# A state-space block and a gated two-layer network: the first weights held back, x issued between GpSimd's own work, and two pieces of weights in one transfer

## The chip, the cores and the metric

The kernel runs on one core of a Trainium2 chip. A core has five engines with instruction queues of their own: TensorE (PE in the profile, with its weight loads as PEld), VectorE (DVE), ScalarE (ACT), GpSimd (POOL) and SyncE (SP), which only issues transfers. Matrix products go to PSUM, everything else lies in SBUF. Transfers from and to the main memory can be issued by SP, ACT and POOL, and are carried by 16 DMA engines.

The metric is the device time of one execution in microseconds; lower is better. The kernel before was run three times: 350.02, 350.31 and 350.38 us, a median of 350.31.

## The reference

The first half is a state-space layer (Mamba-2's SSD) over 4 batches, 8 heads, 768 positions, head size 32 and state size 16, in chunks:

```python
cum = np.cumsum(log(clip(a, 1e-6, 1)), axis=-1)          # inside a chunk
M   = (C @ B^T) * exp(cum_i - cum_j) * causal            # scores, weighed
y   = M @ x  +  (C @ state) * exp(cum)                   # inside, and from earlier chunks
state = exp(sum) * state + sum_j B_j x_j exp(cum_last - cum_j)
```

The second half takes y as 3072 rows of 256 numbers:

```python
h = x @ w_in                        # 256 -> 2048
g = h * (1 / (1 + exp(-1.702 * h)))
out = g @ w_out                     # 2048 -> 256
```

The weights `w_in` and `w_out` come as float64; x, a, B and C as float32. The kernel works in float32.

## The kernel before, in words

The positions are cut into six groups of 128, and a group holds 512 rows of the second half (128 positions of 4 batches). A group consists of two pairs of batches (`PG` = 2), so pair 0 and pair 1 are the batches 0 and 1, and 2 and 3, of the first group. All instructions are written out in one order for each engine, and `in_order` at the end fixes that order; nothing is left to a scheduler but the waits between engines. The change lies in the first 25 us or so, where the first group's state-space part is computed and the first weights come in.

What that beginning consists of, with lines of the kernel before:

- **Loading a, C and B.** One copy of a (L273), eight transfers of C (SP and ACT), eight of B (three by SP, five by POOL; L130).
- **x of the two pairs** is loaded by POOL, two transfers of 128 KB for each pair (`load`, L146), behind POOL's constants: `ident`, `below`, and `pick`, which is one memset and four selects (L287 to L290).
- **Decays.** PE and ACT make `L`, the exponents of the differences of cumulated logarithms, pair 0 with one ACT instruction and pair 1 with four (L531). `drop_of` (L454, POOL) copies the last column of each L, from which `ends_first` (L460, VectorE) makes `Be`, B scaled with the decay to the end of the half chunk.
- **Turning and scores.** `turn_blocks` (L543, VectorE) turns C and B; `turn_back` (L557, PE) turns B back into a PSUM bank, from which `Be` is made; `score` (L599, PE) makes C times B into the area `cb`.
- **Weighing.** `weigh` (L610, VectorE) multiplies L with the scores in place, one half of a pair in an instruction (`k` = 0 and 1).
- **y.** `finish` and `gain` on PE: a dense filler matmul (L418), then products of the weighed L and x (L726, four sets of 16 for each pair), the state's increment from x and `Be` (L630), S on ACT (L646), the products with the state (L711), and the copies to `yT` on ACT (L738).
- **since_start** (L585, POOL) makes C scaled with the decay from the start, read by L711. `first` (L1077) is a POOL memset of a constant that is first read much later, by `clip_rows`.

The weights come in ten **pieces** (`PIECES`, L150): pieces 0 to 3 are two row blocks of 128 of `w_in` each (512 KB of float64), 4 and 5 four row blocks each (1 MB), 6 to 9 are `w_out`. `fetch` (L159) issues a piece as two transfers, one for each half of the inner dimension. Pieces 0 and 1 share a tile, and so do 2 and 3; there are four such tiles. With `held`, a one-element memset of the tile is put on VectorE ahead of the transfer, so that SP waits until VectorE has come to that place.

VectorE and ACT turn a piece into float32: `fields` (L189, L192) splits exponent and mantissa, `clamp` (L201, L203, ACT) moves the exponent, `rounded` (L207) adds the low word, `join` (L221, L227) puts sign, exponent and mantissa together into `w_in` or `w_out`. `narrow(i)` is `rounded(i)`, `fields(i + 1)`, `join(i)`. `join` also fetches a later piece (`NEXT`).

The hidden layer of the first group (`hidden`, L787) goes through 16 row blocks f, each of which needs its part of `w_in`: piece 0 for f = 0 and 1, piece 1 for 2 and 3, piece 2 for 4 and 5, piece 3 for 6 and 7, piece 4 for 8 to 11, piece 5 for 12 to 15. Between the row blocks stand the conversions of the later pieces (`narrow(3)` behind f = 3, `narrow(4)` behind f = 4) and the work of the second group. `az1` and `az` are two more copies of a (64 and 96 KB, L1089 and L1090), which POOL clips (`clip`, L362), and which `pick_a` (L374, ACT) and the store to a scratch area (L1120) read; behind the clips POOL issues the loads of C and B of the second group.

After the first group the kernel is an almost unbroken row of matmuls to the end.

Of the kernel before, what the change touches and what calls it, by code (L numbers as in the profile page):

```python
# [35 lines left out]
def kernel(  # L36
# [73 lines left out]
    cum = const.tile([P, 2, P], FP32, name="cum")  # L110
    w_in = const.tile([P, NF, NK, P], FP32, name="w_in")
    w_out = const.tile([P, 2, NF, P], FP32, name="w_out")
    rx, rb = {}, {}

    blocks = {}

# [17 lines left out]
    def load(p, parts=None, queue=nc.sync):  # L134
        if parts is None:
            parts = "bx"
            if p % PG == 0:
                for name in "CB":
                    load_blocks(p // PG, name, [nc.sync])
        for part in parts:  # L140
            dst, src, e = {"b": (rb, B, N), "x": (rx, x, D)}[part]
            dst[p] = raw.tile([P, 2, NH, e], FP32, tag=part, name=f"{part}{p}", bufs=3)
            for k in range(2):
                c, b = place(p)
                sl = slice(c * P, (c + 1) * P)
                queue.dma_start(out=dst[p][:, k], in_=src[b + k, :, sl, :].rearrange("h s d -> s h d"))  # L146
# [9 lines left out]
    def words(name):  # L156
        return wide.tile([P, 2 * PN], U32, tag="bits", name=name, bufs=BUFS)

    def fetch(i, queue=nc.sync, held=False):  # L159
        name, f, n = PIECES[i]  # L160
        if n == 2 and f % 4:
            t = pieces.pop(i - 1)[:, 2 * n * DM:]
        else:
            t = pieces[i] = words(f"bits{i}")
            t = t[:, :2 * n * DM]
        if held:
            nc.vector.memset(t[:, :1], 0)
        if name == "in":
            src = moe_w_in[:, 2 * f * P:2 * (f + n) * P].rearrange("(k p) e -> p k e", p=P)
            dst, src = (v.rearrange(s, h=n, e=2 * P) for v, s in (  # L170
                (t, "p (h k e) -> k p h e"), (src, "p k (h e) -> k p h e")))
        else:
            src = moe_w_out[f * P:(f + n) * P, :].rearrange("(f p) (h e) -> h p f e", p=P, h=2)
            dst = t.rearrange("p (h f e) -> h p f e", h=2, f=n)
        for k in range(2):
            queue.dma_start(out=dst[k], in_=src[k])  # L176
        t = t.rearrange("p (e w) -> p e w", w=2)
        bits[i] = t[:, :, 0], t[:, :, 1]

# [100 lines left out]
                                compare_op=ALU.is_ge, fill=-1e5, base=0,  # L282
                                channel_multiplier=-1)
    load_blocks(0, "B", [nc.gpsimd, nc.sync, nc.gpsimd, nc.sync, nc.gpsimd, nc.sync, nc.gpsimd, nc.gpsimd])
    fetch(0)
    pick = const.tile([P, NB, Q], FP32, name="pick")
    nc.gpsimd.memset(pick, 1.0)  # L287
    for r in range(R):
# [1 line left out]
        nc.gpsimd.affine_select(out=rows, in_=rows, pattern=[[-NH, NB], [-1, Q]],  # L290
                                compare_op=ALU.is_equal, fill=0.0, base=-Q * r,
                                channel_multiplier=1)
    for p in range(PG):
        load(p, "x", nc.gpsimd)
    early = const.tile([P, 1], FP32, name="early")
    nc.vector.memset(early, 1.0)

# [164 lines left out]
        BE[p] = t.rearrange("p r (k q) n -> p k r (q n)", k=2), t  # L462

    since = {}

    firsts = {}

    def clip_rows(g):
        t = raf[g]
# [49 lines left out]
    def decay_exp(p, r, t):  # L519

        n = 2 * Q * H
        if p not in flat:
            if r is None:
                L = ssd.tile([P, R, n], FP32, tag="L", name=f"L{p}", bufs=3)
            else:
                both = const.tile([P, R, n + P], FP32, name=f"L{p}")
                flat[p, "rows"], L = both, both[:, :, :n]
                since[0] = both[:, :, n:]
            flat[p] = L
            Ls[p] = L.rearrange("p r (k q i) -> p k r q i", k=2, q=Q)  # L530
        nc.scalar.activation(flat[p] if r is None else flat[p, "rows"][:, r], t, AF.Exp)  # L531
# [145 lines left out]
    def finish(pairs, steps=range(2)):  # L677


        g, first = divmod(pairs[0], PG)  # L680
        early = pairs[0] < PG
        if 0 in steps:
            if early:
                banks = begun_y["banks"] = [bank(f"y0_{i}") for i in range(4)]
                y = [t[:, :2 * P].rearrange("p (k i) -> p k i", i=H) for t in banks]
                begun_y[0] = [[y[2 * t + i] for t in range(NK)] for i in range(2)], set()
            else:
                both = area(f"y{pairs[0]}")[:, :, :len(pairs) * 2 * H].rearrange(
                    "p (s t) (k i) -> p s t k i", s=2, i=H)
                begun_y[pairs[0]] = [[both[:, i, t] for t in range(NK)] for i in range(2)] + [both], set()  # L690
        y, begun = begun_y[pairs[0]]

        def begin(i, t, parts):
            new = not begun & {(i, t, q) for q in parts}
            begun.update((i, t, q) for q in parts)
            return new

        def inter(n, p, ts=range(2)):

            b = place(p)[1]  # L700
            for k in range(2):
                for i in range(2):
                    if g == 0 and i == 0:
                        continue
                    old = (state[g][:, 0] if i else state[g - 1][:, 1])[:, b + k]
                    for r in range(R):
                        t = r // 2
                        if t not in ts:
                            continue
                        rows, to = slice(32 * r, 32 * r + 32), Q * D * (r % 2)  # L710
                        nc.tensor.matmul(  # L711
                            out=y[i][t][to:to + Q * D, 2 * n + k], lhsT=old[rows],
                            rhs=st[p]["CsT"][rows, k, SIDES[i]],
                            start=begin(i, t, range(Q * (r % 2), Q * (r % 2) + Q)), stop=early,
                            tile_position=(32 * r, to), skip_group_check=True)

        def intra(n, p):
            L = Ls[p]
            for k, t in [(k, t) for t in range(NK) for k in range(2)] if early else [
                    (k, t) for k in range(2) for t in range(NK)]:  # L720
                if p == 0 and (k, t) == (0, 1):
                    dense(begun_y["banks"][0][:, 2 * P:])
                for q in range(HB):
                    h = t * HB + q
                    for i, side in enumerate(SIDES):
                        nc.tensor.matmul(  # L726
                            out=y[i][t][D * q:D * q + D, 2 * n + k], lhsT=rx[p][side, k, h],
                            rhs=L[side, k, h // Q, h % Q],
                            start=begin(i, t, (q,)), stop=not early, tile_position=(H * i, D * q),
                            skip_group_check=True)  # L730

        cols = slice(2 * first * P, 2 * (first + len(pairs)) * P)

        if first == 0 and g not in yT:
            yT[g] = ffn.tile([P, NK, TG], FP32, tag="yT", name=f"yT{g}")
        if early:
            def copied(i, t):
                nc.scalar.activation(  # L738
                    yT[g][:, t, cols].rearrange("p (k s i) -> p s k i", s=2, i=H)[:, i], y[i][t],
                    AF.Copy)  # L740

            if 0 in steps:
                dense(begun_y["banks"][0][:, 2 * P:])
                intra(0, pairs[0])
                return
            intra(1, pairs[1])
            for t in range(NK):
                copied(0, t)
            for t in range(NK):
                for n, p in enumerate(pairs):  # L750
                    inter(n, p, (t,))
                copied(1, t)
        else:
            for step in steps:
                for n, p in enumerate(pairs):
                    (inter, intra)[step](n, p)
            if 1 not in steps:
                return
            for i in range(2):
                nc.scalar.activation(  # L760
                    yT[g][:, :, cols].rearrange("p t (k s i) -> p s t k i", s=2, i=H)[:, i], y[2][:, i],
                    AF.Copy)
        state.pop(g - 1, None)
        for p in pairs:
            st.pop(p)
            Ls.pop(p)
# [296 lines left out]
    turn_blocks(0, "C")  # L1063
    mask_blocks(1)
    decay_exp(0, None, both[:, :, :2 * Q * H])
    mask_first(0)
    differ_of(1)
    rows_first(seconds)
    for r in range(R):
        decay_exp(1, r, seconds[r][:, :3 * P])  # L1070
    table(AF.Silu)
    drop_of(0)
    drop_of(1)
    for p in range(PG):
        since_start(p, nc.gpsimd)
    firsts[0] = ssd.tile([P, NB, P], FP32, tag="first", name="first", bufs=1)
    nc.gpsimd.memset(firsts[0], 0.0)  # L1077
    turn_blocks(0, "B")
    turn_back()
    fold_ident(1)  # L1080
    score(range(PG))
    fields(0)
    clamp(0)
    for p in range(PG):
        ends_first(p)
    weigh(0, (slice(0, 1),))
    fetch(1, held=True)
    rows = a.rearrange("b h s -> (b h) s")
    nc.sync.dma_start(out=az1[:, 0], in_=rows[:, P:2 * P].unsqueeze(0).to_broadcast([R, NB * NH, P]))  # L1089
    nc.sync.dma_start(out=az.rearrange("p c s -> p (c s)"), in_=rows)  # L1090
    for t in az1, az:
        clip(t)
    weigh(0, (slice(1, 2),))
    for i in range(2, 6):
        fetch(i, held=i == 2)
    for k in range(2):
        weigh(1, (slice(k, k + 1),))
    rounded(0)
# [246 lines left out]
```

## Time and profile before

| | |
|---|---|
| median of three runs | 350.31 us |
| the profiled execution: its own time, its span | 350.15 us, 348.4 us |
| TensorE clock granted in it | 0.999 |
| PE busy | 341.9 us (98%) |
| VectorE busy | 256.5 us (74%) |
| ACT, POOL busy | 149.6 us (43%), 45.6 us (13%) |
| first matmul of the hidden layer (L787) | at 17.09 us |
| share of PE in the chain that ended last | 91% |

A busy PE is not a PE at its peak, since matmuls are pipelined and their ends are modelled. Rows of the timeline are: start in us from the beginning of the span, duration in us (of several instructions merged, from the first start to the last end), engine, line, operation, output and inputs with sizes, count, and in square brackets the idle time of the engine before the row with what ended it. Rows of the chain are start, duration and what; "issue" is time in which nothing that the profile shows was waited for. In the windows by stage, DMA throughput is given in GB/s.

### The profile page before, as it was taken

How to read it: one execution, taken by the hardware profiler on the slowest of the kernel's cores; microseconds unless marked ns; L12 is line 12 of the kernel's file. 1: busy time of each engine (PE TensorE's matmuls, PEld its weight loads, DVE VectorE, ACT ScalarE, POOL GpSimd, SP SyncE). 2: the span in 40 equal slices, each digit the busy share in tenths (PEclk: the TensorE clock that was granted, in tenths of full speed). 3: DMA queues.
4: the chain of work that ended last, by engine and by line, in shares of the span. 5: the costliest groups of instructions: out<-in, count | busy, mean ns of one | idle time of the engine just before them, and what ended most of it. 6: DMA issues, size and time to landing. Idle time of an engine off the chain costs nothing.

```text
span 348.4 us, 8535 instructions
## 1 busy us (share of the span) xinstructions
PE 341.9 (98%) x3514; PEld 280.4 (80%) x3514; DVE 256.5 (74%) x474; ACT 149.6 (43%) x333; POOL 45.6 (13%) x82
## 2 busy tenths in 40 slices
PE   8899999999999999999999999999999999999996
PEld 7557874545788888888888888888888888899996
DVE  7799999999699997839985648985554654455463
ACT  6759774005354313744342543433444321554320
POOL 8446500300495000000000000000000000000000
PEclk9999999999999999999999999999999999999999
DMA  5589984623639000464122326120000120000221
GB/s 137 171 267 312 297 156 129 93 57 73 103 76 149 2 0 13 84 121 92 27 36 58 49 79 120 23 33 8 2 2 2 19 32 11 1 2 0 33 31 60
DMA packets 82831, 25.79 MB, mean 74 GB/s; under 512 B 68856, under 2 KB 81144, under 8 KB 82792
## 3 DMA queue, kind: packets, MB, share of 16 engines
q1 hardware_dynamic: 79912, 23.19, 30.8%
q0 software_dynamic: 1888, 1.74, 2.3%
q8 instruction: 27, 0.44, 0.6%
q10 hardware_dynamic: 992, 0.33, 0.4%
q14 instruction: 12, 0.10, 0.1%
HBM read 21.99 MB, written 3.24 MB: 72 GB/s over the span
## 4 chain that ended last, share of the span: by engine, by line
PE 91%; POOL 2%; DMA 2%; DVE 2%; SPq 1%; issue 1%; POOLq 0%; DVEq 0%
PE acc L945 28%; PE X L843 19%; PE Y L853 14%; PE o L885 8%; PE h L787 7%; PE acc L952 7%; DMA bits<-in_moe_w_in_dram 2%; PE y L726 2%; PE cb L599 2%; PE y L711 2%; PE A L630 1%; POOL x L146 1%; SPq L176 1%; POOL zB L130 1%; DVE L L610 0%
## 5 line engine op out<-in xcount | busy, mean ns | idle before, releaser
L848 ACT ACTIVATE ac<-X 128x256 f32<-128x256 f32 x76 | 29.2, 384 | 79.8 <-PE X L843 79.4
L945 PE MATMUL acc<-mg,mw 128*128 128x256 f32 x192 | 54.5, 379 | 0.0
L972 DVE TENSOR_TENSOR gT<-Y,ac 128x512 f32<-128x512 f32 x38 | 26.2, 690 | 37.4 <-PE Y L853 33.6
L820 ACT ACTIVATE gT<-gT 128x512 f32<-128x512 f32 (+1 forms) x76 | 39.4, 521 | 31.7 <-DVE gT L972 31.1
L843 PE MATMUL X<-my,mi 128*128 128x256 f32 x152 | 45.1, 379 | 0.0
L972 DVE TENSOR_TENSOR gT<-Y,b 128x256 f32<-128x256 f32 x38 | 15.8, 418 | 34.4 <-PE Y L853 34.4
L945 PEld LDWEIGHTS acc<-mg,mw 128*128 128x128 f32 x192 | 36.5, 190 | 5.0
L787 PE MATMUL h<-yT,w_in 128*128 128x128 f32 (+2 forms) x182 | 37.0, 359 | 0.7 <-DVE zC L127 0.4
L945 PE MATMUL acc<-gT,w_out 128*128 128x256 f32 x128 | 35.5, 379 | 0.0
L787 PEld LDWEIGHTS h<-yT,w_in 128*128 128x128 f32 x182 | 26.5, 191 | 10.0 <-issue 6.4
L843 PEld LDWEIGHTS X<-my,mi 128*128 128x128 f32 x152 | 28.0, 190 | 3.8
L885 PE MATMUL o<-gT,w_out 128*128 128x512 f32 x64 | 28.6, 597 | 0.0
L811 DVE TENSOR_TENSOR mg<-gT 128x512 f32<-128x512 f32 x40 | 27.2, 680 | 0.0
L945 PEld LDWEIGHTS acc<-gT,w_out 128*128 128x128 f32 x128 | 24.2, 190 | 3.4 <-ACT yT L760 0.2
L848 ACT ACTIVATE b<-X 128x256 f32<-128x256 f32 x38 | 14.6, 385 | 20.3 <-PE X L843 19.9
L843 PE MATMUL X<-yT,w_in 128*128 128x256 f32 x76 | 23.2, 389 | 0.0
L853 PE MATMUL Y<-yT,w_in 128*128 128x256 f32 x76 | 22.7, 381 | 0.0
L853 PE MATMUL Y<-my,mi 128*128 128x256 f32 x76 | 22.6, 379 | 0.0
L843 PE MATMUL X<-my,w_in 128*128 128x256 f32 x76 | 22.6, 381 | 0.0
L853 PE MATMUL Y<-yT,mi 128*128 128x256 f32 x76 | 22.4, 379 | 0.0
L885 PEld LDWEIGHTS o<-gT,w_out 128*128 128x128 f32 x64 | 11.8, 190 | 13.2 <-issue 12.7
L1004 POOL DMA_DIRECT2D out_dram<-ob x32 | 17.4, 551 | 26.7 <-DVE ob L999 26.1
(140 smaller groups left out, 577.6 us busy)
## 6 DMA issues: line engine op xcount, KB each, us to landing
a<-scratch SPq DMA_DIRECT2D x18, 256.0 KB
bits<-in_moe_w_out_dram SPq DMA_DIRECT2D x8, 512.0 KB
x<-in_x_dram SPq DMA_DIRECT2D x20, 128.0 KB
bits<-in_moe_w_in_dram SPq DMA_DIRECT2D x8, 256.0 KB
bits<-in_moe_w_in_dram SPq DMA_DIRECT2D x4, 512.0 KB
out_dram<-ob SPq DMA_DIRECT2D x128, 16.0 KB
af<-in_a_dram SPq DMA_DIRECT2D x20, 64.0 KB
zC<-in_C_dram SPq DMA_DIRECT2D x36, 32.0 KB
```

The source lines that it names most:

```text
L599: nc.tensor.matmul(out=s["cb"][side, r, k].rearrange("p (q i) -> p q i", q=Q), lhsT=BT[rows, k, side], rhs=CT[rows, k, :, side], start=Tru ...
L787: nc.tensor.matmul(out=h[:, cols], lhsT=w_in[:, f, k], rhs=yT[g][:, k, cols], start=(k == 0 and e == 0), stop=(k == NK - 1), skip_group_ch ...
L811: nc.vector.tensor_tensor(out=t[:, 0:2], in0=B[:, :, 1], in1=B[:, 0], op=ALU.subtract)
L820: nc.scalar.activation(o, i, AF.Silu, scale=GELU_SCALE)
L843: nc.tensor.matmul(out=s["X"], lhsT=lhsT, rhs=rhs, start=i == "1", stop=i == "4", skip_group_check=True)
L848: nc.scalar.activation(copy, s["X"], AF.Copy)
L853: nc.tensor.matmul(out=o, lhsT=lhsT, rhs=rhs, start=s.pop("new", False), stop=i != "5", skip_group_check=True)
L885: nc.tensor.matmul(out=o[c], lhsT=w_out[:, c, f], rhs=gT[g, f // 2][:, f % 2], start=(f == 0), stop=(f == NF - 1), skip_group_check=True)
L945: nc.tensor.matmul(out=acc[g][0][i], lhsT=w, rhs=h, start=(j == 0 and (i, 0) in begins), stop=(j == NF // 2 - 1), skip_group_check=True)
L952: nc.tensor.matmul(out=o[k] if type(o) is list else o[:, cols], lhsT=h[:, cols], rhs=w, start=(j == 0 and (i, k) in begins), stop=(j == NF ...
L972: nc.vector.tensor_tensor(out=o, in0=v, in1=w, op=ALU.add)
L1004: (nc.sync if g else nc.gpsimd).dma_start(out=rows[:, b, :, cols], in_=t[32 * r:32 * r + 32, b * P:(b + 1) * P].rearrange("p (u e) -> p u ...
```

## The change

Seven edits, all at the beginning:

1. `fetch(0)` is issued behind a one-element memset of its tile on POOL, which stands between the third and the fourth select of `pick`; `held` now names the engine of the memset.
2. `first` is made by POOL ahead of the first load of x, and not behind `since_start`.
3. POOL issues x of pair 0, then copies the drop of pair 0, then issues x of pair 1, then copies the drop of pair 1.
4. PE makes the scores ahead of turning B back.
5. VectorE makes `Be` behind the weighing of pair 0 and not ahead of it.
6. Piece 2 is fetched as four row blocks, in two transfers of 512 KB in place of four of 256 KB; its second half serves as piece 3. Pieces 1, 2, 4 and 5 are issued ahead of the two copies of a (`az1`, `az`).
7. The second dense filler of pair 0's y stands ahead of the set (1, 0) and not (0, 1), that is behind the first set and not the second.

```diff
-    def fetch(i, queue=nc.sync, held=False):
+    def fetch(i, queue=nc.sync, held=None):
         name, f, n = PIECES[i]
+        if i == 2:
+            n = 4
...
         if held:
-            nc.vector.memset(t[:, :1], 0)
+            held.memset(t[:, :1], 0)
...
         bits[i] = t[:, :, 0], t[:, :, 1]
+        if i == 2:
+            for j in range(2):
+                bits[i + j] = tuple(v[:, 2 * j * DM:2 * (j + 1) * DM] for v in (t[:, :, 0], t[:, :, 1]))
...
-    fetch(0)
     pick = const.tile([P, NB, Q], FP32, name="pick")
...
                                 compare_op=ALU.is_equal, fill=0.0, base=-Q * r,
                                 channel_multiplier=1)
-    for p in range(PG):
-        load(p, "x", nc.gpsimd)
+        if r == 2:
+            fetch(0, held=nc.gpsimd)
+    firsts[0] = ssd.tile([P, NB, P], FP32, tag="first", name="first", bufs=1)
+    nc.gpsimd.memset(firsts[0], 0.0)
+    load(0, "x", nc.gpsimd)
...
-                if p == 0 and (k, t) == (0, 1):
+                if p == 0 and (k, t) == (1, 0):
                     dense(begun_y["banks"][0][:, 2 * P:])
...
     decay_exp(0, None, both[:, :, :2 * Q * H])
+    drop_of(0)
+    load(1, "x", nc.gpsimd)
     mask_first(0)
...
     table(AF.Silu)
-    drop_of(0)
     drop_of(1)
     for p in range(PG):
         since_start(p, nc.gpsimd)
-    firsts[0] = ssd.tile([P, NB, P], FP32, tag="first", name="first", bufs=1)
-    nc.gpsimd.memset(firsts[0], 0.0)
     turn_blocks(0, "B")
+    score(range(PG))
     turn_back()
     fold_ident(1)
-    score(range(PG))
     fields(0)
     clamp(0)
+    weigh(0, (slice(0, 1),))
+    fetch(1, held=nc.vector)
+    weigh(0, (slice(1, 2),))
+    for i in (2, 4, 5):
+        fetch(i, held=nc.vector if i == 2 else None)
     for p in range(PG):
         ends_first(p)
-    weigh(0, (slice(0, 1),))
-    fetch(1, held=True)
     rows = a.rearrange("b h s -> (b h) s")
     nc.sync.dma_start(out=az1[:, 0], in_=rows[:, P:2 * P].unsqueeze(0).to_broadcast([R, NB * NH, P]))
     nc.sync.dma_start(out=az.rearrange("p c s -> p (c s)"), in_=rows)
     for t in az1, az:
         clip(t)
-    weigh(0, (slice(1, 2),))
-    for i in range(2, 6):
-        fetch(i, held=i == 2)
     for k in range(2):
         weigh(1, (slice(k, k + 1),))
```

More of the change, by code (lines that the diff above doesn't have):

```diff
@@ L112 @@
     w_out = const.tile([P, 2, NF, P], FP32, name="w_out")
-    rx, rb = {}, {}
+    rx, rb, firsts = {}, {}, {}
     blocks = {}
@@ L464 @@
     since = {}
-    firsts = {}
     def clip_rows(g):
```

## The prediction

> **What bounds the kernel now.** I read the page first (PE busy 98% of the span), then the chain of waits, then the timeline of each engine from 0 to 50 us, because every edit sits there. After 29.43 us the chain runs through PE almost alone, so what PE gains or loses before that point should carry to the end.
>
> The chain of waits, in order of time (start, us, what):
>
> ```profile
> 10.65 0.81 DVE Be L460 x2
> ...
> 13.37 0.68 DVE L L610
> ...
> 18.35 8.22 DMA bits<-in_moe_w_in_dram
> 26.66 0.69 DVE p L189
> ...
> 28.59 0.69 DVE w_in L227
> ...
> 29.43 3.69 PE h L787 x16
> ```
>
> The same place in PE's timeline, and the start of the hidden layer:
>
> ```profile
> 15.54 0.46 PE L726 MATMUL y<-L,x 64*32 64x64 f32 x32 [0.41 <-ACT S L646]
> ...
> 17.09 9.39 PE L787 MATMUL h<-yT,w_in 128*128 128x512 f32 x30 [0.19 <-ACT yT L738]
> ...
> 26.99 1.99 PE L787 MATMUL h<-yT,w_in 128*128 128x256 f32 x8
> 29.43 7.40 PE L787 MATMUL h<-yT,w_in 128*128 128x256 f32 x32 [0.44 <-DVE zC L127]
> ```
>
> So between 17.09 and 48 us PE loses one visible piece, 0.44 us ahead of row block f=6. The releaser named, the memset of zC, is a bystander: w_in for f=6 is written by L227 at 28.59, which ends at 29.28. VectorE's rows tell why it is late:
>
> ```profile
> 10.65 0.81 DVE L460 TENSOR_TENSOR Be<-b,drops 128x256 f32<-128x256 f32 x2 [0.77 <-POOL drops L454]
> 11.54 1.30 DVE L610 TENSOR_TENSOR L<-L,cb 128x512 f32<-128x512 f32 x2
> ...
> 18.33 1.31 DVE L207 SCALAR_TENSOR_TENSOR m<-bits,m 128x512 f32<-128x512 uint32 x1
> 19.56 0.41 DVE L221 SCALAR_TENSOR_TENSOR p<-bits,p 128x256 uint32<-128x256 uint32 x1
> ...
> 20.35 0.97 DVE L189 TENSOR_SCALAR p<-bits 128x512 uint32<-128x512 uint32 x1
> ...
> 22.36 0.68 DVE L207 SCALAR_TENSOR_TENSOR m<-bits,m 128x512 f32<-128x512 uint32 x1
> ...
> 26.66 0.69 DVE L189 TENSOR_SCALAR p<-bits 128x1024 uint32<-128x1024 uint32 x1 [0.88 <-DMA bits<-in_moe_w_in_dram]
> ```
>
> Three things are to be seen: 0.77 us of waiting for the drops at 9.9, 0.88 us for piece 4 at 25.8, and two rows that are slow against their likes (1.31 against 0.68; 0.97 against 0.42) while GpSimd clips az:
>
> ```profile
> 6.60 3.77 POOL L146 DMA_DIRECT2D x<-in_x_dram x4
> 10.41 0.20 POOL L454 COPY drops<-L 128x16 f32<-128x16 f32 x1
> ...
> 18.27 2.77 POOL L362 TENSOR_SCALAR az<-az 32x768 f32<-32x768 f32 x1
> ```
>
> The windows by stage give 224 GB/s from 13 to 17 us, 262 from 17 to 20, 175 from 20 to 23, and 359 from 23 to 28.
>
> **Part 1: GpSimd's queue.** Between the third and fourth select of `pick` comes a one-element memset (0.10, row of `pick`), ahead of x the 0.53 us memset of `first`. The first x of pair 0 is issued at 7.4 instead of 6.60, its second at 8.3 instead of 7.5. Then drop 0 (0.20, its L is ready at 8.72), then pair 1's x at 9.5 and 10.4 instead of 8.4 and 9.3, drop 1 near 11.6 instead of 10.8, the two CsT until 12.6 instead of 11.84. CsT is read at 15.92: hidden by 3 us. x takes 3.3 to 4.2 us to land (median 3.7): pair 0 at 11.1 and 12.0, at worst 11.6 and 12.5; pair 1 at 13.2 and 14.1, at worst 14.6. Its readers come below.
>
> **Part 2: the first weights.** `fetch(0)` waits for the memset, which ends near 6.54: 6.58 instead of 4.92. Its landing is not shown. In before it was used at 9.13 without a wait, so it takes at most 4.2 us; x's quickest, 3.3, is the lower end: landed between 9.9 and 10.8. I take 10.5, nearer its own row. In before `fields(0)` ran at 9.13 in the shade of the wait for the drops; now it is what VectorE waits for. What is queued behind it: the weighing, the rest of `bits`, everything.
>
> **Part 3: VectorE's order.** Scores go ahead of the turning back of B, so PE starts them when `cb` is free (L531 of pair 0 ends at 8.72) and the last L490 is done, near 9.1, and not at 10.23; with 1.21 us they end at 10.3. `fields(0)` 10.55 to 11.3 (0.76, as 9.13 to 9.89), the first weighing 11.35 to 12.0. Before: 11.54. Gain about 0.2. The second ends at 12.65 (12.84 before); then both Be (0.81), which stood ahead of the weighing, 12.7 to 13.5; pair 1's weighing to 14.75 (14.05 before). That is late by 0.7, read below.
>
> **Part 4: PE up to the hidden layer.** First y at 12.05, the dense filler (0.70) now stands behind the first group, second group near 13.0, third and fourth at 13.5. The third takes the bank that the Be rows read, so it can't go before 13.5; in before it went at 13.80. Then gain (0.7) to 14.3, with pair 1's x at 14.1 just in time; ScalarE's S (0.63) to 15.0; meanwhile pair 1's first half ends at 15.0 behind the weighing of 14.75. Second half at 15.1 instead of 15.54, and from there as before (1.55 to h): h starts at 16.7 instead of 17.09. Bounds: landing of piece 0 at 9.9 gives 0.5 earlier (then x holds), at 10.8 with x at 14.6 it gives 0.1 later. I take 0.35 earlier. w_in for f=0 is ready at 16.2 (rows 13.96 to 15.44, moved by 0.7): 0.5 in hand.
>
> **Part 5: SyncE's queue.** Piece 1 is issued at 12.0 instead of 12.28. Behind it now come piece 2 (two DMAs of 512 KB for four of 256), 4 and 5, and az last. Piece 2 starts at 13.3 instead of 14.75, and 160 KB of az (64 and 96) are out of its way: 0.7 us at 224 GB/s. VectorE meets piece 1 at 16.4 instead of 16.76. Its rows from 16.76 to 25.78 take 9.02 us, of which 1.17 were the slow ones (0.62 and 0.55), gone from here as az is not there yet: it comes to piece 4 at 24.3. Both halves of piece 2 must land before `fields(2)` at 19.4: 1 MB from 15.0 at 224 to 262 GB/s is there between 19.1 and 19.8; f=4 is ready by 23.3 and PE wants it at 24.0. Cost nothing, and 0.7 in hand.
>
> **Part 6: piece 4.** It landed at 26.57. Lower bound of the shift: 0.3 (issue of piece 1) and 0.7 (az), 1.0; upper: with piece 2 moving at the 359 GB/s of the 512 KB DMAs, a further 1.5. I take 2.0, so 24.6. Then f=6 is ready 2.62 later (26.66 to 29.28), at 27.3, and PE wants it at 28.6: the 0.44 goes entirely. What is late next is f=8, ready at 32.99 in before, 6.33 after the start of `fields(4)`; PE wanted it at 33.13. Now it is 24.65 + 6.33 = 31.0, plus what the clip of az costs, which now comes when az lands behind piece 5, about 27.5 to 31.4, over the rows of pieces 4 and 5: the same 1.17, bounds 0 and 2.77. So 32.2, and PE wants it at 33.13 - 0.35 - 0.44 = 32.3. Just hidden.
>
> az's other readers: `pick_a` at 34.31, the scratch store at 34.64, free. The block loads on GpSimd behind the clip start near 31.5 instead of 29.60; B of block 1, last issued at 40.68, is read at 51.76. Hidden.
>
> **Sum.** 0.35 + 0.44 = 0.8 less, in the profiled execution 350.15 - 0.8 = 349.35; that execution is 0.16 under the median, so **349.5**.
>
> **Rivals.**
> A, the forecast: front 0.1 worse to 0.5 better, and the 0.44: 349.4 to 350.0; with the scatter of the runs shown (0.36) 349.2 to 350.1.
> B, the front gains nothing: x of pair 1 lands at 14.6, or piece 0 after 10.8, so h starts at 17.1; and piece 4 at 25.2 makes f=8 ready at 32.75. Gain 33.13 - 32.75 = 0.4: 349.9. For it: x is issued 1.1 us later. Against it: the gain step wants the last x only at 14.1.
> C, slower: f=8 becomes the wait. Place: VectorE between `fields(4)` and the first `join(4)`. Price: with piece 4 at 26.57 as before, f=8 is ready at 26.66 + 6.33 + 1.17 = 34.16, 1.0 later than PE had it: 351.3. It decides once piece 4 lands after 33.13 - 7.5 = 25.6. For it: 20 to 23 us moves 175 GB/s, which I can't explain and which may stay. Against it: az and the later issue are gone.
>
> D, the clip holds VectorE for the whole 2.77: f=8 is ready at 31.0 + 2.77 = 33.8, 0.6 later than PE had it: 350.9. Against it: L221 at 19.56 ran in its usual 0.41 inside the clip, and the two slow rows lost 1.17 together.
> The Trainium skill, "SBUF — State Buffer", section "Who interferes with whom", has D's rule: a VectorE instruction with two SBUF inputs beside a GpSimd one that reads SBUF contends for a shared read interface, and the one that comes second is blocked entirely, not slowed. By it the sum would be D's and not A's; the trace agrees that such rows are slowed and disagrees that all are held.
>
> **Chances.** A 0.52, B 0.26, C 0.17, D 0.05. About 0.2% (0.7 us) can be told from no change: 349.6 and below is faster, 351.0 and above slower. Of A 0.05 lies above 349.6, B and D are within (D just), C is slower and D's upper end with it: faster 0.47, same 0.33, slower 0.20. Range 348.9 (front 0.5, the 0.44, and half a us for waits after 48 us that I have not followed) to 351.3 (C).
>
> **What would show it.** First weighing near 11.3; h near 16.7; no gap at f=6; VectorE's wait for piece 4 short or gone; L207 or L189 slow after 27 and not at 18; f=8 without a gap. Wrong if `fields(0)` waits past 11, or if PE waits for L227 near 33.

## The result, and the profile after

The changed kernel takes 352.76 us (median of four, 352.30 to 353.44), the kernel before beside it 350.35 (350.02 to 350.45): a ratio of 1.0087, 95% interval 1.0070 to 1.0103. It is slower by 2.4 us. The forecast of 349.5 was wrong in sign, and the time lies outside its range. The profiled execution took 352.30 us (span 350.6), against 350.15 (348.4).

The chain of waits after the change (start, us, what), for the same stretch as before:

```profile
6.83 0.13 SPq L178
7.00 5.21 DMA bits<-in_moe_w_in_dram
12.30 0.09 DVE p L194
...
13.07 0.60 DVE L L615 x2
...
14.96 0.18 SPq L178
15.18 8.42 DMA bits<-in_moe_w_in_dram
23.69 0.43 DVE p L194
...
32.26 1.31 DVE p L194
...
34.81 0.70 DVE w_in L232
35.65 3.69 PE h L792 x16
```

Lines have moved by five or so: L194 is `fields`, L615 the weighing, L232 `join`, L792 the hidden layer. The chain now begins with the held transfer: its second half is issued at 7.00 and lands 5.21 us later, at 12.21. Counted from the first issue, at 6.57, that is 5.64 us, where the prediction took at most 4.2. Then the chain goes through the weighing, behind which the merged piece 2 is issued, through that transfer (8.42 us) and through VectorE's conversions to row block f = 8. VectorE's timeline has the same two waits, and the rows at the clip:

```profile
12.30 0.43 DVE L194 TENSOR_SCALAR p<-bits 128x512 uint32<-128x512 uint32 x1 [3.14 <-DMA bits<-in_moe_w_in_dram]
12.64 0.42 DVE L197 TENSOR_SCALAR m<-bits 128x512 uint32<-128x512 uint32 x1
12.98 1.29 DVE L615 TENSOR_TENSOR L<-L,cb 128x512 f32<-128x512 f32 x2
...
23.69 0.43 DVE L194 TENSOR_SCALAR p<-bits 128x512 uint32<-128x512 uint32 x1 [1.42 <-DMA bits<-in_moe_w_in_dram]
...
28.50 0.69 DVE L194 TENSOR_SCALAR p<-bits 128x1024 uint32<-128x1024 uint32 x1
...
32.26 1.31 DVE L194 TENSOR_SCALAR p<-bits 128x1024 uint32<-128x1024 uint32 x1
```

`fields(0)` runs at 12.30 and not at 10.55, the first weighing at 12.98 and not at 11.35; `fields(2)`, which needs piece 2, runs at 23.69 (before: 20.35, in the prediction's rows). PE's timeline shows what follows:

```profile
10.74 0.60 PE L425 MATMUL y<-ones 128*128 128x256 f32 x2
13.72 0.35 PE L731 MATMUL y<-L,x 64*32 64x64 f32 x16 [2.38 <-DVE bits L169]
...
17.94 1.61 PE L716 MATMUL y<-CsT,S 32*64 32x64 f32 x32
19.54 9.99 PE L792 MATMUL h<-yT,w_in 128*128 128x512 f32 x30
...
30.05 5.45 PE L792 MATMUL h<-yT,w_in 128*128 128x256 f32 x24
35.65 3.69 PE L792 MATMUL h<-yT,w_in 128*128 128x256 f32 x16 [0.15 <-DVE w_in L232]
```

PE stands for 2.38 us ahead of the first y, and the hidden layer starts at 19.54 instead of 17.09. The row of L716 took 0.97 before and takes 1.61 now. The windows by stage say why (busy time of PE, PEld, DVE, ACT, POOL; granted clock; DMA share; GB/s):

```profile
10.00:15.00 5.00, 2.62 (x58) 1.49 (x44) 2.70 (x9) 3.38 (x6) 2.15 (x5) 1.00 0.51 125
15.00:18.00 3.00, 2.66 (x129) 2.25 (x128) 2.97 (x7) 0.90 (x3) 0.00 (x0) 0.50 0.85 243
18.00:22.00 4.00, 4.00 (x37) 2.54 (x36) 2.23 (x6) 2.48 (x5) 0.00 (x0) 0.52 0.96 288
22.00:25.00 3.00, 3.00 (x8) 1.33 (x7) 1.54 (x5) 0.82 (x2) 0.00 (x0) 1.00 1.07 364
```

From 15.0 to 21.8 us PE's granted clock is half; before it was 1.00 in all four windows. GpSimd did what Part 1 wrote:

```profile
7.34 1.81 POOL L146 DMA_DIRECT2D x<-in_x_dram  x2
9.20 0.20 POOL L461 COPY drops<-L 128x16 f32<-128x16 f32 x1
9.35 1.77 POOL L146 DMA_DIRECT2D x<-in_x_dram  x2
...
31.85 3.11 POOL L369 TENSOR_SCALAR az<-az 32x768 f32<-32x768 f32 x1
```

PE's own account up to f = 8, which starts 35.65 - 33.13 = 2.52 later: first y 13.72 against 12.29, 1.43 late; y to the hidden layer 5.82 against 4.80, 1.02 more; row blocks 0 to 4 (to the start of f = 5) 10.51 against 9.90, 0.61 more; from there to f = 8 5.60 against 6.14, 0.54 less, since the gap of 0.44 at f = 6 is gone and one of 0.15 at f = 8 has come. That is 2.52. The two middle terms, 1.6, lie where the clock is half.

VectorE's account gives the same 2.52, and it is the one that the chain of waits follows: `fields(2)` starts 23.69 - 20.35 = 3.34 later, and the rows from there to the `w_in` of f = 8 take 11.82 (to 35.51) against 12.64 (to 32.99), 0.82 less. The two ways end within 0.15 us of each other, so taking away the half clock alone would not have brought f = 8 forward.

### The profile page after: what moved, and what is told of

It reads as the page before. It is cut to its first block, busy times and chain, and to the rows that moved or that the text cites. A ratio compares the mean times of both kernels' runs of the same rounds, so it can differ in the third digit from the quotient of the medians.

```text
span 350.6 us, 8532 instructions
## 1 busy us (share of the span) xinstructions
PE 343.2 (98%) x3514; PEld 282.1 (80%) x3514; DVE 255.9 (73%) x474; ACT 149.3 (43%) x333; POOL 45.0 (13%) x83
## 4 chain that ended last, share of the span: by engine, by line
PE 89%; DMA 4%; DVE 3%; POOL 2%; issue 1%; SPq 0%; POOLq 0%; DVEq 0%
PE acc L950 28%; PE X L848 19%; PE Y L858 14%; PE o L890 8%; PE acc L957 7%; PE h L792 6%; DMA bits<-in_moe_w_in_dram 4%; PE y L731 2%; PE cb L604 2%; PE y L716 2%; PE A L635 1%; POOL zB L130 1%; DVE p L194 1%; DVE m L197 1%; DVE p L226 1%
## 5 line engine op out<-in xcount | busy, mean ns | idle before, releaser
L825 ACT ACTIVATE gT<-gT 128x512 f32<-128x512 f32 (+1 forms) x76 | 39.3, 519 | 31.9 <-DVE gT L977 31.2
L792 PE MATMUL h<-yT,w_in 128*128 128x128 f32 (+2 forms) x182 | 37.4, 364 | 0.2 <-DVE w_in L232 0.2
L792 PEld LDWEIGHTS h<-yT,w_in 128*128 128x128 f32 x182 | 27.3, 194 | 9.1 <-issue 6.7
L890 PEld LDWEIGHTS o<-gT,w_out 128*128 128x128 f32 x64 | 11.8, 190 | 13.2 <-issue 12.7
```

What stands on the lines that cost most here:

```text
L792: nc.tensor.matmul(out=h[:, cols], lhsT=w_in[:, f, k], rhs=yT[g][:, k, cols], start=(k == 0 and e == 0), stop=(k == NK - 1), skip_group_ch ...
L825: nc.scalar.activation(o, i, AF.Silu, scale=GELU_SCALE)
L890: nc.tensor.matmul(out=o[c], lhsT=w_out[:, c, f], rhs=gT[g, f // 2][:, f % 2], start=(f == 0), stop=(f == NF - 1), skip_group_check=True)
```

## The experiments

All comparisons are with runs of the kernel before on the same chip, whose median there was 349.3 to 350.0. The ratios are given with their 95% intervals; where times inside a run are given, they are of its one profiled execution. Single executions scatter more there (348.8 to 353.2 for the kernel before).

**A queue that the prediction did not look at.** The page's list of queues has, before and after, a row for instructions:

```profile
q8 instruction: 27, 0.44, 0.5%
```

These are 27 packets of 16 KB, 0.44 MB in all, for 7028 instructions of PE on the page (3514 products and as many weight loads). By that an instruction has some 63 bytes and a packet some 260 instructions; this is an estimate. A packet takes 0.9 to 1.7 us, once 2.4 (e2). I call one a refill. The Trainium skill, "Runtime: NRT & Kernel Launch", section "Instruction fetch mechanics", has such blocks of 256 instructions fetched on a queue of the engine's own, and says that this is hidden behind the issue of instructions. The trace agrees with the block and, as will be seen, not with the hiding. The packets' times are in the trace itself, and no view lists them. Here they are beside piece 0 (two transfers, each of 16 shares that land one by one):

| kernel | 2nd issue of piece 0, took | first refill | 15 of its 16 shares, last one | PE idle ahead of y | hidden layer | executions with a mean clock up to 0.995 |
|---|---|---|---|---|---|---|
| before | 5.40, 0.47 | 8.21 to 9.18 | 8.78, 8.83 | 0.22 | 17.09 | 7 of 90 |
| after | 7.00, 1.63 | 7.04 to 8.24 | 12.15, 12.21 | 2.38 | 19.54 | 4 of 4 |
| e1 no hold | 5.48, 0.47 | 8.43 to 9.37 | 8.67, 10.98 | 0.26 | 17.36 | 1 of 10 |
| e2 hold only | 7.04, 1.35 | 7.04 to 8.00 | 12.62, 12.89 | 3.10 | 21.04 | 4 of 4 |
| e3 15 pads | 7.00, 0.47 | 7.57 to 9.18 | 10.14, 11.69 | 2.34 | 19.15 | 10 of 10 |
| e4 earlier hold | 6.40, 0.47 | 7.01 to 8.40 | 9.88, 10.92 | 1.28 | 17.39 | 3 of 10 |
| e5 4 fillers | 7.00, 1.32 | 7.01 to 7.95 | 11.95, 13.10 | 2.19 | 20.43 | 3 of 8 |
| e7 no hold, no merging | 5.55, 0.47 | 8.70 to 9.67 | 8.89, 9.14 | none | 17.38 | 1 of 10 |
| e9 x by SP | 7.07, 1.54 | 7.27 to 8.23 | 11.29, 11.68 | 1.81 | 18.32 | 6 of 10 |
| e12 hold, early refill | 7.09, 0.47 | 3.16 to 4.43 | 10.40, 10.48 | none | 23.57 | 4 of 4 |
| e13 order and az | 5.54, 0.47 | 7.90 to 8.89 | 8.79, 8.90 | none | 16.56 | 0 of 12 |

Where a refill covers the issue, the issue ends 0.4 us after the refill does (8.63 after 8.24, 8.39 after 8.00). Where the issue was free of it but a refill ran about the time that the data came, one share can land 1.0 to 2.3 us behind the other fifteen (e1, e3, e4). That does not always happen: in before, e7 and e13 a refill ran beside piece 0's last shares as well, and none was late. There it is the first transfer of x whose last share is 0.7 to 1.0 us behind (in before 10.85, with fifteen there by 9.82). That such a share stands behind the refill on one DMA engine would fit, and is not shown.

**e1: the hold taken away.**

```diff
+    fetch(0)
     pick = const.tile([P, NB, Q], FP32, name="pick")
...
-        if r == 2:
-            fetch(0, held=nc.gpsimd)
```

> The changed kernel with the first weights issued as before (ahead of pick, no memset on GpSimd); all the rest of the change stays. Theory H (the held first weights are the loss: their second half landed at 12.21 us and everything on VectorE waited): back to the kernel before or a little under it, 349.3 to 350.3, fields(0) without a wait, hidden layer starting at 16.5 to 17.1. Rival M (the merged transfer, az behind the pieces, or the order of x are the loss): stays at 352 to 353.

350.9 us, ratio 1.0021 (0.9996 to 1.0046). The hold is most of the loss (0.66 of the 0.87% in the ratios), but what is left gains nothing. PE's timeline has two new gaps:

```profile
8.78 0.94 PE L603 MATMUL cb<-CT,Bt 32*64 32x128 f32 x43
10.81 0.66 PE L603 MATMUL cb<-CT,Bt 32*64 32x128 f32 x21 [1.09 <-issue]
...
17.36 5.42 PE L791 MATMUL h<-yT,w_in 128*128 128x512 f32 x14 [0.19 <-ACT yT L742]
23.83 3.89 PE L791 MATMUL h<-yT,w_in 128*128 128x256 f32 x16 [1.04 <-DVE w_in L232]
```

The scores stop after 43 of 64 products for 1.09 us with nothing to wait for that the profile shows ("issue"). The refill, behind piece 0's data, ended at 9.37, and PE goes on 1.44 later. The same happens 1.59 behind the refill of 9.67 in e7 (a gap of 0.96) and 1.35 behind that of 16.48 in e11 (1.18). So piece 0 and the refill meet: with the hold piece 0 is second, without it PE is. The 1.04 at f = 4 is the merged piece 2, whose second half lands at 22.03.

**e2: the kernel before with the hold alone.**

```diff
-    fetch(0)
...
+        if r == 2:
+            fetch(0, held=nc.gpsimd)
```

> The kernel before with nothing but the first weights held by the memset on GpSimd behind the third select. H: the second transfer of piece 0 is held up in its issue again, lands near 12, 351.5 to 352.8. M: 350.0 to 350.6, because the cover of the drops is still there.

354.51 us, ratio 1.0116 (1.0069 to 1.0164). The hold alone loses more than the whole change; y starts 2.77 later than before, and the chain of waits runs on from there through PE, 5.98 us from y to the hidden layer where it was 4.80:

```profile
15.06 0.35 PE L727 MATMUL y<-L,x 64*32 64x64 f32 x16 [3.10 <-DVE bits L167]
```

**e3: 15 warm-up pads and not 31** (32 products fewer on PE, so the refill is asked for later).

```diff
-    pads(31, busy)
+    pads(15, busy)
```

> The changed kernel with 15 tiny warm-up matmuls on PE in place of 31, so that PE comes to its refill of instructions some 64 instructions later. Theory R (the issue of the second half of piece 0 was held from 7.00 to 8.63 us by the 16 KB instruction packet that ran from 7.04 to 8.24): that issue takes 0.5, the piece lands near 10.5 instead of 12.2, time 349.8 to 351.0. Rival X (the issue is slow because GpSimd generates x's transfers at the same time, from 7.34): unchanged, 352.3 to 353.2, the issue still takes 1.6.

352.56 us, ratio 1.0085 (1.0055 to 1.0115): the issue takes its usual 0.47, as the theory said, but the last share lands at 11.69 all the same, and nothing is won. The stalled issue is then not the whole of the lateness; in this execution a late share (11.69, with fifteen there by 10.14) makes up the rest.

**e4: the hold two selects earlier** (`if r == 0`).

> The changed kernel with the memset that holds piece 0 behind the first select of pick and not the third: piece 0 is issued near 5.95 us instead of 6.57, so both issues are over before TensorE's instruction refill of 7.0 us. Theory (the landing follows from the time of issue, because data asked for ahead of the refill and ahead of x keeps its place): last landing near 10.3 us instead of 12.21, fields(0) near 10.5, TensorE idle ahead of y for about 1 us instead of 2.38, h near 17.2, 350.0 to 350.8. Rival (any hold at all costs what the late one costs, through x's transfers): fields(0) at 11.5 or later, h at 19 or later, 352 or more.

350.74 us, ratio 1.0022 (0.9993 to 1.0051). The second issue, 0.6 earlier, is over before the refill starts; the last share lands 1.3 earlier (10.92), the hidden layer starts 2.15 earlier (17.39), with a clock of 1.00 in the profiled execution. The ratio is 0.65% under that of the changed kernel, 2.3 us for a shift of 0.6: the transfer gets past the refill, and in seven of ten executions PE keeps its clock. PE waits 0.41 us for `w_in` at f = 8, which starts at 33.52.

**e9: x issued by SP, behind piece 0.**

```diff
-    load(0, "x", nc.gpsimd)
+    load(0, "x", nc.sync)
```

and the same for pair 1.

> The changed kernel with the four transfers of x issued by SyncE behind piece 0, and none by GpSimd; piece 0 is still held, until about 6.6 us or a little before. Theory S (x of the same time takes the DMA engines from piece 0): x now stands behind piece 0, so its last half lands near 10.5 us instead of 12.21, although the refill still covers its second issue. x lands later, near 13 to 14.5, and y waits for that. Rival (the landing is late for a reason that has nothing to do with x): last landing 11.7 or later as in the changed kernel. The end says less than the landing: 352 to 353.5 by either, as x holds y back.

351.95 us, ratio 1.0063 (1.0036 to 1.0089). Without GpSimd's transfers beside it the last share still lands at 11.68, behind an issue that stood for 1.54: the rival. Transfers of x cost piece 0 0.5 us at the most.

**e5 and e10: PE kept busy ahead of y**, with 4 and with 8 fillers instead of one.

```diff
-                dense(begun_y["banks"][0][:, 2 * P:])
+                for _ in range(8):
+                    dense(begun_y["banks"][0][:, 2 * P:])
```

> The changed kernel with four dense filler matmuls in place of one ahead of the first y, so that PE does not idle from 11.3 to 13.7 us and its clock is not halved from 15 to 22 us. Theory W (the weights' chain sets f=8: PE waited for it even with the slow clock): hidden layer starts 0.8 to 1.2 earlier, f=8 hardly moves, time 352.3 to 352.8. Rival K (the halved clock is about half of the loss): 351.3 to 351.8.

> The changed kernel with eight dense filler products (0.43 us each) ahead of the first y and not one, so that TensorE stays busy from 10.7 to about 14 us while the first weights come. Theory (some 1 us of the loss is that TensorE, idle for 2.4 us, gets half of its clock from 15 to 22 us): no row of half clock between 15 and 22, y to h 4.8 us as before the change and not 5.8, h near 18.8 if y starts at 14.1, time 351.5 to 352. Rival (the low clock follows from the work that comes then, not from the idle time): the clock is half again, y to h 5.8, h near 19.9, 353.

e5: 353.17 us, ratio 1.0073 (1.0038 to 1.0108). Piece 0 landed at 13.10, PE still idled for 2.19, the clock still fell in the profiled execution: it does not decide between the two. e10, PE's timeline:

```profile
10.79 3.62 PE L425 MATMUL y<-ones 128*128 128x256 f32 x16
...
17.77 0.97 PE L716 MATMUL y<-CsT,S 32*64 32x64 f32 x32
18.93 5.42 PE L793 MATMUL h<-yT,w_in 128*128 128x512 f32 x14 [0.19 <-ACT yT L743]
25.32 3.89 PE L793 MATMUL h<-yT,w_in 128*128 128x256 f32 x16 [0.96 <-DVE w_in L232]
...
35.56 3.69 PE L793 MATMUL h<-yT,w_in 128*128 128x256 f32 x16 [0.40 <-DVE w_in L232]
...
263.51 0.21 PE L731 MATMUL y<-L,x 64*32 64x64 f32 x1 [1.75 <-issue]
```

With PE busy the granted clock is 1.00 up to 26 us, L716 is back at 0.97, and y to the hidden layer takes 18.93 - 14.34 = 4.59 and not 5.82. The idle time is the cause of the half clock: the theory. But the whole clock, which makes up for y's start 0.62 later, buys next to nothing at f = 8: PE waits 0.96 us at f = 4 for piece 2, which lands at 23.52 (23.59 in the changed kernel), and 0.40 at f = 8, which starts at 35.56 and not 35.65. That is what theory W of e5 said: the weights' chain sets f = 8. And the time, 355.44, ratio 1.0144 (1.0091 to 1.0198), misses both expectations. Up to 50 us e10 is level with the changed kernel (`project` at 50.62 and 50.71); the loss comes with two gaps of "issue" later, 0.65 at 208 and 1.75 at 263, the second followed by 3.4 us of half clock. The seven more fillers are 28 more instructions for PE; the refills now fall at other places of the program. The trace has refills that end at 207.63 and 262.15, 1.28 and 1.36 us before PE goes on after the two gaps, about as in e1, e7 and e11: the gaps are refills that came too late.

**e11 and e12: the refill brought forward**, by 67 pads in place of 31 and shorter fillers behind them, without the hold and the merging (e11) and in the changed kernel as it is (e12).

```diff
-    pads(31, busy)
+    pads(67, busy)
...
-        dense(both[:, r, 2 * P:], 3, False)
+        dense(both[:, r, 2 * P:], 1, False)
```

> The changed kernel without the hold and with pieces 2 and 3 apart (the run of 349.76 us beside 349.33 before the change), with 67 warm-up pads in place of 31 and shorter fillers behind them, so that TensorE asks for its next 256 instructions near 5.3 us and not near 7. Theory R (one refill of TensorE's instructions and piece 0 meet in the DMA engines, and whichever is second costs a microsecond: with the hold it is piece 0, without it TensorE, which stands for 0.96 us in the middle of the scores): the refill now runs ahead of most of piece 0; no stall in the scores, scores over near 10.2 and not 11.9, fields(0) before them without a wait, first weighing near 11.0 and not 12.03, h near 16.5 and not 17.38; 0.5 to 0.9 us less than that kernel, a ratio to before of 0.996 to 0.998. Rival (the stall in the scores has another cause, or the refill only moves the wait): a stall of about 1 us again at the scores or elsewhere before 12 us, h near 17.3, ratio 0.999 to 1.002.

> The changed kernel with 67 pads in place of 31 and shorter fillers behind them: the hold stays, the refill comes ahead of the issue of piece 0 (near 5.3 to 6.4 us). Theory R: the second issue of piece 0 takes its usual 0.47 us and no share of it waits for a refill: all landed near 10.0 us and not 12.21, fields(0) near 10.2, TensorE idle under 1 us ahead of y, no half clock from 15 to 22, h near 17.0 and not 19.54, and about 1.5 to 2.5 us less than the changed kernel (352.76). Rival (the landing is late by x's transfers or by the hour of the issue): landed at 11.5 or later, h at 19 or later, no gain.

What they were made for, they show. In e12, with the hold and x as in the changed kernel, the second issue takes 0.47 and piece 0 is there at 10.48 and not 12.21, with no straggler, and VectorE hardly waits:

```profile
10.58 0.70 DVE L194 TENSOR_SCALAR p<-bits 128x512 uint32<-128x512 uint32 x1 [0.44 <-DMA bits<-in_moe_w_in_dram]
```

e12 also issues pair 1's x 0.8 us later, but e9, with no transfer of x from GpSimd beside piece 0, gained 0.5 at the most. So the refill is what made the held transfer late, by far the most of it. As times they failed, 358.1 (1.0243, 1.0222 to 1.0264) and 359.45 (1.0262, 1.0216 to 1.0307). Two things were not reckoned with. PE was slow early on: from 6 us the decays' products take 1.16 and 1.24 where they took 0.69 and 0.73. The trace's records of the clock begin with a full one only at 10.9 (e11) and 12.6 us (e12), against 6.6 before the change, and there too a row ahead of that is slow (0.98 at 5.95, the like at 7.51 0.69). So the clock was presumably still low, for the smaller warm-up work; the records do not show it. And the later refills moved too: in e12 the third, at 19.37, came in the midst of the transfers of pieces 1 to 5, and PE had nothing to execute until 1.3 us after its end:

```profile
21.61 0.43 PE L731 MATMUL y<-L,x 64*32 64x64 f32 x7 [4.29 <-issue]
```

**e7: no hold, and pieces 2 and 3 apart** (`for i in range(2, 6)`, without the lines for `i == 2` in `fetch`).

> The changed kernel without the hold (piece 0 issued at 5.0 us as before the change) and with pieces 2 and 3 as separate transfers of 256 KB each, still ahead of the two copies of a. Beside the kernel without the hold alone (350.9) it tells the merging. Theory (the wait of 1.04 us at f = 4 there comes from piece 2 being there only when all of its 1 MB is): piece 2 lands near 19.5, no wait at f = 4, 349.6 to 350.0. Rival (that wait comes from the order of the queue or from contention, not from the merging): VectorE waits over 1 us for piece 2 again, 350.6 or more.

349.76 us, ratio 0.9993 (0.9963 to 1.0023). No wait at f = 4, so that wait was the merging's; f = 6 has no gap, f = 8 has 0.66.

**e8: edits 4, 5 and 7 alone**, on the kernel before.

```diff
+    score(range(PG))
     turn_back()
     fold_ident(1)
-    score(range(PG))
```

with `ends_first` behind the weighing of pair 0 and the filler ahead of the set (1, 0).

> The kernel before with edits 4, 5 and 7 alone: scores ahead of turning B back, Be behind the weighing of pair 0, the second filler behind the first set. Theory R: the scores start near 9.1 but TensorE runs out of instructions in them while the refill waits behind piece 0 (start 8.2 to 8.7), a stall near 1 us; first weighing 11.9 to 12.1, h 17.2 to 17.4, ratio to before 1.000 to 1.002. Rival (what the prediction worked out for these edits): scores over at 10.3, first weighing 11.35, h 16.7, ratio 0.998 to 0.999.

350.11 us, ratio 1.0008 (0.9993 to 1.0022). Neither theory: no long stall in the scores, but one share of piece 0 came at 10.86 and held the weighing until 11.65; the gap at f = 6 stayed (0.53).

**e6b and e14: az behind the pieces, alone**, on the kernel before; e14 is the same kernel with more executions.

> The kernel before with only the two copies of a moved behind pieces 2 to 5 in SyncE's queue, pieces 2 and 3 apart as before. Theory (what the prediction says of az): piece 4 lands about 0.7 us earlier, near 25.9; no gap or 0.1 at f = 6 instead of 0.44; the clip falls over the rows of pieces 4 and 5, two of which take 1.3 instead of 0.7, and f = 8 waits 0.3 to 0.7: a wash, ratio 0.999 to 1.001. Rival (the clip costs nothing there): both gaps gone, ratio 0.9985 or less.

> The kernel before with only az moved behind the pieces, as in the run of 350.0 us, in five rounds. Theory: the 0.44 us at f = 6 goes and f = 8 keeps its place, ratio 0.998 to 0.9992. Rival: a wash, since in most executions the wait turns up at f = 8: ratio 0.9995 to 1.001.

350.0 us, ratio 1.0008 (0.9979 to 1.0037), and 349.49, ratio 0.9997 (0.9974 to 1.0019). PE's timeline of e6b has no gap at f = 6 nor at f = 8, and its span is 347.6, but neither comparison tells it from no change:

```profile
17.43 8.90 PE L787 MATMUL h<-yT,w_in 128*128 128x512 f32 x30 [0.19 <-ACT yT L738]
...
26.84 9.16 PE L787 MATMUL h<-yT,w_in 128*128 128x256 f32 x40
```

**e13: both together**, that is the change without the hold, without the new order on GpSimd and without the merging.

> The kernel before with edits 4, 5 and 7 and az behind the pieces; no hold, no merging, x as before. Theory (Parts 3, 4 and 6 of the prediction were right in kind, the hold and the merging lost what they gave): h 0.2 to 0.4 us earlier than in the run beside it, no gap at f = 6, f = 8 with 0.3 to 0.6 of waiting behind the clip; ratio to before 0.997 to 0.999. Rival (f = 8 takes all of it back, as VectorE's rows of pieces 4 and 5 now bound): h earlier but f = 8 at the time of before or later, ratio 0.9995 to 1.001.

348.76 us (348.30 to 351.08, twelve executions) beside 349.88: ratio 0.9969 (0.9946 to 0.9991). This is faster than both kernels. PE and VectorE:

```profile
9.15 0.94 PE L599 MATMUL cb<-CT,Bt 32*64 32x128 f32 x43
10.43 0.66 PE L599 MATMUL cb<-CT,Bt 32*64 32x128 f32 x21 [0.35 <-issue]
...
16.56 8.88 PE L787 MATMUL h<-yT,w_in 128*128 128x512 f32 x30 [0.19 <-ACT yT L738]
...
25.94 9.20 PE L787 MATMUL h<-yT,w_in 128*128 128x256 f32 x40
```

```profile
24.41 0.69 DVE L189 TENSOR_SCALAR p<-bits 128x1024 uint32<-128x1024 uint32 x1 [0.53 <-DMA bits<-in_moe_w_in_dram]
...
30.11 1.19 DVE L227 SCALAR_TENSOR_TENSOR w_in<-m,p 128x512 f32<-128x512 f32 x1
```

The hidden layer starts at 16.56, where the prediction wrote 16.7 for the changed kernel; piece 4 is met at 24.41 (24.6); there is no gap at f = 6 and none at f = 8, although the clip slows a row. These are the two gains that the forecast added up.

## Why the prediction was wrong

**Part 2 failed, and with it the sign.** It bounded the landing of the held weights by 4.2 us, "its own row" in the kernel before, as if that time did not depend on when the transfer is asked for: between 9.9 and 10.8. It was 12.21. PE's first refill goes out at 7.0. In the kernel before it ran only from 8.21, with piece 0's first transfer and part of its second ahead of it, so the row of before contained no trace of it; e2, with the same program on PE and piece 0 later, has it at 7.04. Moved behind 6.5, the transfer meets it, in its issue (1.16 us longer than its usual 0.47) and in its landing. e12 takes the refill out of the way and leaves the hold: 10.48, where the prediction took 10.5. e3 and e4, which move one of the two against the other by half a microsecond, lie between. The sentence that named the condition, "wrong if `fields(0)` waits past 11", is what came true.

**Part 5 failed too**, and lies on the same chain. It had piece 2 there between 19.1 and 19.8 (1 MB from 15.0 at 262 and 224 GB/s is 19.0 to 19.7). It was there at 23.59, and VectorE waited 1.42 us for it. 1.4 us of that is Part 2's: the issue came at 14.72 and not 13.3. The rest is the transfer itself. Piece 1 is landing on the same queue until 17.43, and 1 MB from there to 23.59 is 170 GB/s, while all transfers together moved 288 GB/s from 18 to 22: piece 4, issued from 15.73 on, has its first share at 22.22, ahead of piece 2's last. In e1, 1 MB from 17.11 to 22.03 is 213 GB/s. So the start was two microseconds early in the forecast and the rate too high. Apart, the first two row blocks come earlier, `fields(2)` runs at 20.22, and nothing waits at f = 4 (e7).

In the start of f = 8 the two can be told apart, in one profiled execution each: 33.13 before, 33.10 without hold and merging (e7), 34.04 with the merging (e1), 35.65 with both. The merging costs 0.9 and the hold 1.6.

**What a late start costs was not in any rival.** B allowed for piece 0 after 10.8 and gave 17.1 and 349.9 for it. It left out that the weighing, and so the issue of piece 2, comes late with it, and that a PE that idles loses its clock. The second adds 1.6 us on PE's own way to f = 8; as the weights' chain is as long, it does not add to the 2.5 in this execution. Where the chain of waits runs through PE from the first y, as in e2 and e3, it does count. e10 shows the cause, and the table how often it strikes: where the profiled execution idles for up to 0.3 us ahead of y, one execution in ten or fewer has a lower mean clock (in e6b, not in the table, two of ten); it is three of ten at 1.28, six of ten at 1.81, three of eight at e5's 2.19, and all at 2.34 and above. Idle time ahead of y is not the whole of it: in e11 and e12 PE stands inside y, for 1.18 and 4.29 us, and all executions are low.

**Part 1** was right in order, and near in all but one: x lands at 11.34, 13.11, 13.72 and 14.06 (11.1, 12.0, 13.2, 14.1). The second is 0.6 past its worst of 12.5, off the path as piece 0 was later. **Parts 3 and 4** were right in kind: with piece 0 issued as before, the new order of scores, Be and filler gives 0.5 us at the hidden layer in e13, 0.35 forecast; e13 is not alone in its edits, and e8 alone did not show it in its time.

**Part 6** came out for another reason, by luck. There is no gap at f = 6 and no wait for piece 4, as it said, but piece 4 landed at 26.64 and not 24.6 (26.57 before). `w_in` for f = 6 was ready at 31.11, later than the 29.28 of before and not at 27.3; nothing waits because PE comes to f = 6 only near 31.9 and VectorE to `fields(4)` at 28.50. In e13, without hold and merging, its reasoning holds: piece 4 is met at 24.41. The clip's price was too high: beside it L194 takes 1.31 for 0.69 and another row 0.08 more, 0.7 in place of 1.17, and 0.6 in e13.

**Rival C** had the place right: f = 8 is where VectorE's chain meets PE, ready at 35.51. The wait seen is only 0.15 because PE came late as well. Its reason, a late piece 4, was not the one; piece 2 was. **Rival D** is out: in the changed kernel two-input rows inside the clip (31.85 to 34.96), L226 at 34.09 wholly and L232 at 34.81 in part, took their usual 0.68 and 0.69, and it was a row with one input that slowed. The rule cited there from the Trainium skill ("SBUF — State Buffer", "Who interferes with whom") would have held the former; the trace disagrees, though e13's slow row, L227, does have two inputs.

## What to carry to other kernels

Before a transfer is held back, see what else goes out at the hour it is moved to, and that includes the instructions of the busiest engine: a landing time read at one hour is not a bound at another. Where an engine's idle time ahead of a burst grows, price the burst at the clock it will then have, and see whether another chain is as long: of two ways that end together, shortening one gains nothing. And try the parts of a bundled change apart: here the hold and the merged transfer lost more than the rest gave, and the rest without them and without the new order on GpSimd is 0.3% faster than the kernel before.

## What the runs showed of the hardware

- Instructions come through the same DMA engines as data, 16 KB at a time, and the two delay each other by about a microsecond: an issue on SP ends 0.4 us after a refill that it met, and PE stands ("issue") until 1.3 to 1.6 us after the end of a refill that came late (e1, e7, e10, e11, e12); the longest such gap, 4.29 us, came while the weights were moving (e12).
- Adding or taking away instructions moves all later refills. With 28 more ahead of y, PE stood for 2.4 us at 208 and 263 us, where it had not before (e10).
- PE's granted clock can halve after an idle time that is short: in the profiled executions it did after 2.2 to 3.1 us (after, e2, e3, e5), after 1.75 in e10 and around one of 1.18 in e11; it did not after 1.28 (e4) and 1.81 (e9). It stays so for 3.4 (e10), 6.8 (after, e2, e3, e11, e12) or 10.2 us (e5). The Trainium skill, "TensorE: Matmul & The Clock Gate", section "Part 1: The HAM clock gate", has it fall after an idle window of about 3.4 us that runs freely. The half clock agrees, and so do stretches of one, two and three times 3.4 us; but PE was idle for 3.1 us at most ahead of y, so that a window need not be wholly idle.
